# Query projections over 64 rows in two array halves, and the first expert's second-layer loads, dummy operands and output products moved round the routing

## The chip, the cores and the metric

The kernel runs on one core of one Trainium2 chip. The metric is device time in microseconds (us) of one execution, where lower is better. Times below come from the runs of the kernel before and from one execution of it that the hardware profiler recorded.

## What is computed

Three blocks follow each other over T = 2304 tokens (4 sequences of 576) and 512 channels (8 heads of 64).

```python
def phi(x):                                   # q, k: [4, 8, 576, 64], w_phi: [64, 128]
    proj = np.einsum('bhsd,df->bhsf', x, w_phi)
    proj = proj - np.max(np.abs(proj), axis=-1, keepdims=True)
    return np.concatenate([np.exp(proj), np.exp(-proj)], axis=-1)
q_p, k_p = (phi(q), phi(k))
kv = np.einsum('bhsf,bhsd->bhfd', k_p, v);  z = np.sum(k_p, axis=2)
x = (q_p @ kv) / (q_p @ z + 1e-6)             # linear attention, then [4, 576, 512]
gate = sigmoid(causal_conv5(x, conv_w))
y = (gate * (x @ w_val)) @ w_out              # gated block
e[s] = argmax(y @ w_gate) where sigmoid(y @ w_local) < 0.5 or s == 0, else e[s-1]
out[s] = softmax(y @ w_gate)[e] * (relu(y @ w1[e]) @ w2[e])   # 8 experts, 512 -> 1024 -> 512
```

## The kernel before, in words

Tokens are worked on in 18 tiles of 128. The kernel has five stretches.

**Keys.** For each tile and each half of the heads (`hh`), `proj` (L115) multiplies the raw k by the feature map `wraw`, which holds `w_phi` twice on its diagonal, so that one product of 128 rows (two heads' channels) by 256 columns serves two heads. VectorE takes the largest magnitude (L132, tile `m`) and subtracts it (L134, tile `pp`), ScalarE makes both exponentials, and `kv` (L159) sums keys times values in 64-column products.

**Queries and the gated block.** For q, `split` (L105) first makes a rounded high part of a raw tile on ScalarE (`qkh`) and the rest of it on GpSimd (`qkl`); both are of the type fp32r, which TensorE streams faster than fp32. `proj` then issues three products of 128 rows by 256 columns for each pair of heads: `qkh` by `wb_hi`, `qkh` by `wb_lo`, `qkl` by `wb_hi`, so 6 for each half of a tile and 12 for a tile. The result `pj` of a half fills one bank of PSUM; the pool `ps_p` has two. `tq` transposes (L186, tile `tp`), `nm` (L198, tile `num`) multiplies by the sums of the keys in 64-column products (16 in the program for each half; an fp32 product shows as two records in the trace), `tx` (L225) transposes back, and `conv`, `val` (L400, tile `vps`) and `ymm` (L535, tile `yps`) are the gated block. The program's order on each engine is set by a scheduler that places instructions when the ones they need are ready.

**Routing.** Products of `ymm` that are left over are called one at a time by `yfill(n)` between the short dependent steps that choose experts and build the index tables (L680 to L757). `yfill(999)` puts all that remain ahead of the last of these, `tab`. `pin` keeps those instructions in the program's order.

**Handover.** After `tab`, 30 dummy products (`idle`, L762; operands `ones` and `ohl`, a one-hot table of the routing) keep TensorE busy while the tables are finished. Tiles of the routing and of the gated block then give up their memory to the experts' weights, so that a tile of the experts waits for the last reader of what lay there.

**Experts.** Units of 256 or 384 gathered tokens. `gather` (L815) fetches rows by index on GpSimd's queue; `rows` transposes them (L827, `xp`) and splits them into `xh` and `xl`; `unit` does the first layer (L857, `hp`; `hh` and `hlo` leave it) and the second (L871, `op`). Weights come as 8 pieces of 512 KB for each expert (4 of `w1`, 4 of `w2`; L801, tile `wraw`, 3 buffers, on SP's queue); each piece is split by ScalarE (`w1h`, `w2h`) and VectorE (`w1l`, `w2l`). Before the first unit all 8 pieces of its expert are asked for and split in a row; those of expert i+1 are split at eight points inside unit i (`between`).

Of the kernel before, what the change touches and what calls it, by code (L numbers as in the profile page):

```python
# [8 lines left out]
F32 = mybir.dt.float32  # L9
F32R = mybir.dt.float32r  # L10
# [21 lines left out]
WARM = 30  # L32
# [5 lines left out]
def body(ctx, tc, qT, kT, v1, wbd, w_val, conv_w, w_out, w_gl, w1, w2, out):  # L38
# [42 lines left out]
    wb_hi = ap.tile([128, 256], F32R, name="wb_hi")  # L81
    wb_lo = ap.tile([128, 256], F32R, name="wb_lo")

    raw_t, hl_t, v_t = {}, {}, {}
# [20 lines left out]
    def split(nm, t):  # L105

        if t >= NT or (nm, t) in hl_t or nm == "k":
            return
        hi = ap.tile([128, 4, 128], F32R, tag="qkh", name="qkh", bufs=2)
        lo = ap.tile([128, 4, 128], F32R, tag="qkl", name="qkl", bufs=2)  # L110
        hi_of(A, hi, raw_t[nm, t])
        lo_of(G, lo, raw_t[nm, t], hi)
        hl_t[nm, t] = (hi, lo)

    def proj(nm, t, hh):  # L115
        raw = raw_t[nm, t]
        if nm == "k" and hh == 1:
            pj = ps_b.tile([128, 4, 128], F32, tag="b", name="pj")
        else:
            pj = ps_p.tile([128, 4, 128], F32, tag="pj", name="pj")  # L120
        for cc in range(2):
            c = 2 * hh + cc
            o = pj[:, 2 * cc:2 * cc + 2, :].rearrange("p h f -> p (h f)")
            prods = ((raw, wraw),)
            if (nm, t) in hl_t:
                hi, lo = hl_t[nm, t]
                prods = ((hi, wb_hi), (hi, wb_lo), (lo, wb_hi))
            for i, (st, mv) in enumerate(prods):
                PE.matmul(o, lhsT=st[:, c, :], rhs=mv, start=(cc == 0 and i == 0),  # L129
                          stop=(cc == 1 and i == len(prods) - 1), skip_group_check=True)  # L130
        m = ap.tile([128, 4], F32, tag="m", name="m", bufs=3)
        V.tensor_reduce(m, pj, axis=AX.X, op=ALU.max, apply_absolute_value=True)  # L132
        pp = ap.tile([128, 4, 128], F32, tag="pp", name="pp", bufs=3)
        V.tensor_tensor(pp, pj, m.unsqueeze(2).to_broadcast([128, 4, 128]), ALU.subtract)  # L134
        return pp
# [469 lines left out]
    def run(nbg, rate):  # L605
        n = len(items)
        txq = []
        for i in range(-LF, n + 3):
# [5 lines left out]
            if 0 <= i + LF < n:  # L614
                kind, t, hh = items[i + LF]
                if hh == 0:
                    loads_to(ahead[i] + 3)
                    for z in order[:ahead[i] + 2]:
                        split(*z)
                if kind == "k":  # L620
                    pk(t, hh)
                else:
                    pq(t, hh)
# [19 lines left out]
    hi_of(V, wb_hi, wraw)  # L643
    lo_of(V, wb_lo, wraw, wb_hi)
# [34 lines left out]
    yfill(18)  # L679
# [81 lines left out]
    for _ in range(WARM):  # L761
        pin(PE.matmul(idle, lhsT=rc["ones"], rhs=ohl[:, 0:4, :].rearrange("p t c -> p (t c)"), start=True, stop=True))  # L762
# [48 lines left out]
    def gather(gcols):  # L811
        xs = []
        for gc in gcols:
            xg = fx.tile([128, YW], F32, tag="xg", name="xg", bufs=XG)
            G.indirect_dma_start(out=xg, out_offset=None, in_=y_d, in_offset=bass.IndirectOffsetOnAxis(ap=gc, axis=0))  # L815
            xs.append(xg)
        return xs
# [79 lines left out]
    with tc.issue_after(W["tap"].ins), tc.issue_after(W["tanh"].ins):  # L897
        for p in pieces:
            p()()
    xs = gather(cols(gidx, units[0][0], units[0][1]))  # L900
    cur_x = rows(xs, unit_probs(0))
    xs = {1: gather(cols(gidx, units[1][0], units[1][1]))}
    for i, (c0, n, e) in enumerate(units):
# [3 lines left out]
        if not last:  # L907
            nxt["w"], pieces = unit_weights(i + 1)
            started = [p() for p in pieces[:3]]
            todo = pieces[3:]  # L910

        def between():
            if not last and started:
# [59 lines left out]
```

## Time and profile before

| | us |
|---|---|
| median of 3 runs | 597.88 (596.02 to 600.78) |
| the profiled execution | 596.02 |
| its span, first to last instruction | 594.2 |
| TensorE busy in the span | 569.9 |

The profiled execution is the fastest of the three runs, 1.86 us below their median, and 1.8 us of it lie outside the span. All times of rows count from the span's start. TensorE is PE in rows, its weight loads PEld, VectorE DVE, ScalarE ACT, GpSimd POOL. A matmul's record holds its latency, so records that follow each other overlap: what one costs is the distance from its start to the next one's.

### The profile page before, as it was taken

What the parts mean: (1) busy time and instruction counts of PE and PEld (TensorE: products, weight loads), DVE (VectorE), ACT (ScalarE), POOL (GpSimd) and SP (SyncE); (2) the same over time, 40 slices, a digit from 0 to 9 for tenths busy, and PEclk for the clock granted to TensorE, in tenths of its full rate; (3) what the DMA queues carried; (4) which work ended last, traced back from release to release, by engine and by line L of the source; (5) the groups of instructions that cost most, each with busy time, mean ns of one, the idle gap of its engine ahead of it and who ended that gap; (6) DMA issues with size and microseconds to landing.
All of it is one profiled execution on the core that took longest, in us unless ns stands there. A gap on an engine that the chain in (4) does not pass through costs nothing. (4 is left out here: it accounts for less than half of the span.)

```text
span 594.2 us, 13524 instructions
## 1 busy us (share of the span) xinstructions
PE 569.9 (96%) x5477; PEld 495.5 (83%) x5478; DVE 365.2 (61%) x726; ACT 313.1 (53%) x573; POOL 238.0 (40%) x258
## 2 busy tenths in 40 slices
PE   7999999999999999999997999999999999999993
PEld 6777788898889889888784988889889899898982
DVE  5888689478687876569613766555666656452110
ACT  3767566466665575565323656445655646541210
POOL 2453055388778885583124022322340322311001
PEclk9999999899999999999998899999999999999997
DMA  8934431111101000221524887758668649620000
GB/s 281 311 99 122 130 107 49 32 33 38 36 4 35 3 38 21 72 77 48 198 90 132 302 268 217 239 190 269 210 211 272 202 138 291 203 95 36 17 19 36
DMA packets 46017, 76.82 MB, mean 129 GB/s; under 512 B 3839, under 2 KB 22399, under 8 KB 45952
## 3 DMA queue, kind: packets, MB, share of 16 engines
q1 hardware_dynamic: 39840, 60.55, 32.8%
q0 software_dynamic: 3520, 10.58, 4.7%
q10 hardware_dynamic: 2592, 4.79, 2.1%
q8 instruction: 45, 0.74, 0.5%
q14 instruction: 20, 0.16, 0.1%
HBM read 66.39 MB, written 10.56 MB: 130 GB/s over the span
## 5 line engine op out<-in xcount | busy, mean ns | idle before, releaser
L857 PE MATMUL hp<-xh,w1h 128*128 128x256 f32 (+1 forms) x320 | 94.6, 296 | 1.4 <-DVE hlo L860 0.8
L857 PE MATMUL hp<-xh,w1l 128*128 128x256 f32 (+1 forms) x320 | 93.8, 293 | 0.0
L857 PE MATMUL hp<-xl,w1h 128*128 128x256 f32 (+1 forms) x320 | 93.3, 294 | 0.0
L815 POOL DMA_INDIRECT xg<-y_d,gidx x22 | 36.7, 1669 | 98.5 <-DVE p L838 83.4
L877 POOL DMA_INDIRECT out<-osb,sidx x22 | 28.0, 1271 | 115.1 <-ACT osb L876 69.0
L871 PE MATMUL op<-w2h,hh 128*128 128x512 f32 x176 | 69.5, 400 | 1.0 <-ACT hh L859 0.9
L52 DVE TENSOR_TENSOR w2l<-wraw,w2h 128x1024 fp32r<-128x1024 f32 x40 | 48.8, 1223 | 34.5 <-ACT w2h L49 34.3
L860 DVE SCALAR_TENSOR_TENSOR hlo<-hp,hh 128x256 fp32r<-128x256 f32 (+1 forms) x80 | 34.2, 446 | 55.4 <-ACT hh L859 55.4
L871 PE MATMUL op<-w2l,hh 128*128 128x512 f32 x176 | 68.2, 393 | 0.0
L871 PE MATMUL op<-w2h,hlo 128*128 128x512 f32 x176 | 67.0, 394 | 0.0
L857 PEld LDWEIGHTS hp<-xh,w1h 128*128 128x128 f32 x320 | 61.2, 191 | 3.9 <-DVE hlo L860 1.2
L52 DVE TENSOR_TENSOR w1l<-wraw,w1h 128x1024 fp32r<-128x1024 f32 x40 | 48.7, 1251 | 24.1 <-ACT w1h L49 24.1
L857 PEld LDWEIGHTS hp<-xh,w1l 128*128 128x128 f32 x320 | 61.1, 191 | 1.4
L857 PEld LDWEIGHTS hp<-xl,w1h 128*128 128x128 f32 x320 | 60.7, 191 | 0.0
L132 DVE TENSOR_REDUCE m<-pj 128x4 f32<-128x512 f32 x72 | 49.3, 686 | 18.4 <-PE pj L129 17.5
L266 DVE SCALAR_TENSOR_TENSOR acc<-xT,tfs,acc 128x256 f32<-128x256 f32 (+1 forms) x112 | 53.8, 485 | 10.8 <-ACT acc L264 9.7
L859 ACT ACTIVATE hh<-hp 128x256 fp32r<-128x256 f32 (+1 forms) x80 | 31.4, 403 | 53.8 <-PE hp L857 53.6
L49 ACT CAST w2h<-wraw 128x1024 fp32r<-128x1024 f32 x40 | 41.8, 1050 | 31.7 <-DMA wraw<-w 22.3
L49 ACT CAST w1h<-wraw 128x1024 fp32r<-128x1024 f32 x40 | 40.3, 1049 | 24.6 <-DMA wraw<-w 24.5
L159 PEld LDWEIGHTS kv<-v,ex 128*64 128x64 f32 (+1 forms) x1280 | 40.7, 137 | 14.7 <-issue 6.8
L134 DVE TENSOR_TENSOR pp<-pj,m 128x512 f32<-128x512 f32 x72 | 49.4, 686 | 4.4 <-PE tp L186 1.8
L159 PE MATMUL kv<-v,ex 128*64 128x65 f32 (+1 forms) x1280 | 46.1, 224 | 3.0 <-DVE kvsb L171 1.4
(194 smaller groups left out, 1332.5 us busy)
## 6 DMA issues: line engine op xcount, KB each, us to landing
wraw<-w SPq DMA_DIRECT2D x80, 512.0 KB, 4.5
v<-v SPq DMA_DIRECT2D x18, 260.0 KB, 3.2
y_d<-ysb ACTq DMA_DIRECT2D x18, 260.0 KB, 2.1
raw<-qT SPq DMA_DIRECT2D x18, 256.0 KB, 2.9
raw<-kT SPq DMA_DIRECT2D x17, 256.0 KB, 4.2
wr<-w_val SPq DMA_DIRECT2D x4, 512.0 KB, 5.9
wr<-w_out SPq DMA_DIRECT2D x4, 512.0 KB, 6.9
xg<-y_d,gidx POOLq DMA_INDIRECT x22, 5.4
```

What stands on the lines that cost most here:

```text
L49: (A.copy if eng is A else eng.tensor_copy)(hi, src)
L52: eng.tensor_tensor(lo, src, hi.bitcast(F32), ALU.subtract)
L132: V.tensor_reduce(m, pj, axis=AX.X, op=ALU.max, apply_absolute_value=True)
L134: V.tensor_tensor(pp, pj, m.unsqueeze(2).to_broadcast([128, 4, 128]), ALU.subtract)
L159: PE.matmul(kv_ps[b][blk // 7][mh * 64:mh * 64 + 64, (blk % 7) * VW:(blk % 7 + 1) * VW], lhsT=kp_t[t, hh][off:off + n, sg, h, mh * 64:mh * ...
L266: W["tap"] = V.scalar_tensor_tensor(acc[c], xs, cw[:, kk, c:c + 1], acc[c], ALU.mult, ALU.add)
L815: G.indirect_dma_start(out=xg, out_offset=None, in_=y_d, in_offset=bass.IndirectOffsetOnAxis(ap=gc, axis=0))
L857: PE.matmul(hp[:, 0:n], lhsT=wt[:, k, f * 128:(f + 1) * 128], rhs=xt[:, k, 0:n], start=(i == 0), stop=(i == 11))
L859: A.activation(hh[:, f, 0:n], hp[:, 0:n], AF.Relu)
L860: low = V.scalar_tensor_tensor(hlo[:, f, 0:n], hp[:, 0:n], 0.0, hh[:, f, 0:n].bitcast(F32), ALU.max, ALU.subtract)
L871: PE.matmul(op, lhsT=ht[:, f, sl], rhs=wt[:, f, :], start=(i == 0), stop=(i == 23))
L877: G.indirect_dma_start(out=out, out_offset=bass.IndirectOffsetOnAxis(ap=scols[j], axis=0), in_=osb, in_offset=None, bounds_check=T - 1, oo ...
```

## The change

Four things change.

1. The query projection uses raw fp32 operands and no split. The host orders the heads so that a block of 128 channels holds head c in rows 0 to 63 and head c+4 in rows 64 to 127. At the first half of a tile, 8 products of 64 rows by 128 columns are written, alternating between the upper and the lower half of the rows (`z`), into both banks of `ps_p`. The 18 ScalarE casts `qkh`, the 18 GpSimd subtractions `qkl` and the two splits of `wraw` go.
2. `yfill(18)` becomes `yfill(24)` ahead of the first routing transpose.
3. The 30 dummy products of 512 columns become 60 of 256 columns, with the identity matrix as both operands.
4. The first expert's `w2` pieces are asked for behind the first gather and split inside the first unit; the next expert's pieces start two `between` points later.

```diff
-    def split(nm, t):
-        if t >= NT or (nm, t) in hl_t or nm == "k":
-            return
-        hi = ap.tile([128, 4, 128], F32R, tag="qkh", name="qkh", bufs=2)
-        lo = ap.tile([128, 4, 128], F32R, tag="qkl", name="qkl", bufs=2)
-        hi_of(A, hi, raw_t[nm, t])
-        lo_of(G, lo, raw_t[nm, t], hi)
-        hl_t[nm, t] = (hi, lo)
+    def products(nm, t, hh):
+        raw = raw_t[nm, t]
+        if nm == "k":
...
+        elif hh == 0:
+            for z in range(2):
+                pj_t[z] = ps_p.tile([128, 4, 128], F32, tag="pj", name="pj")
+            for c in range(4):
+                for z in range(2):
+                    rows = slice(z * 64, z * 64 + 64)
+                    PE.matmul(pj_t[z][:, c, :], lhsT=raw[rows, c, :], rhs=wraw[rows, z * DF:z * DF + DF],
+                              start=(c == 0), stop=(c == 3), skip_group_check=True)
     def proj(nm, t, hh):
...
-            if (nm, t) in hl_t:
-                hi, lo = hl_t[nm, t]
-                prods = ((hi, wb_hi), (hi, wb_lo), (lo, wb_hi))
...
+        products(nm, t, hh)
+        pj = pj_t.pop(hh)
...
-    yfill(18)
+    yfill(24)
...
-        pin(PE.matmul(idle, lhsT=rc["ones"], rhs=ohl[:, 0:4, :].rearrange("p t c -> p (t c)"), start=True, stop=True))
+        pin(PE.matmul(idle[:, 0:256], lhsT=ident.bitcast(BF16)[:, 0:128], rhs=ident.bitcast(BF16), start=True, stop=True))
...
-        for p in pieces:
+        for p in pieces[:4]:
             p()()
     xs = gather(cols(gidx, units[0][0], units[0][1]))
+
+    with tc.issue_after(W["gather"].ins):
+        late = [p() for p in pieces[4:7]]
+    late_todo = pieces[7:]
...
-            started = [p() for p in pieces[:3]]
-            todo = pieces[3:]
+            started = [p() for p in pieces[:0 if i == 0 else 3]]
+            todo = pieces[len(started):]
 
         def between():
-            if not last and started:
+            if late:
+                for _ in range(2):
+                    late.pop(0)()
+                    if late_todo:
+                        late.append(late_todo.pop(0)())
+                if not late:
+                    started.extend(todo.pop(0)() for _ in range(3))
+            elif not last and started:
```

On TensorE, early in the query stretch, a half of a tile had six products of the same shape before (the number in a name tells tiles of one name apart):

```order
L198 MATMUL num_1478<-kvsb_526,ex_1434 64x65 x16
L129 MATMUL pj_1599<-wb_hi_94,qkh_1414 128x256
L129 MATMUL pj_1599<-wb_lo_95,qkh_1414 128x256
L129 MATMUL pj_1599<-wb_hi_94,qkl_1415 128x256
L129 MATMUL pj_1599<-wb_hi_94,qkh_1414 128x256
L129 MATMUL pj_1599<-wb_lo_95,qkh_1414 128x256
L129 MATMUL pj_1599<-wb_hi_94,qkl_1415 128x256
L186 MATMUL tp_1546<-ident_61,pp_1427 128x128 x4
```

At the same place of the changed kernel, the two results of one tile (`pj_1507` from the upper rows of `raw_1270`, `pj_1508` from the lower) stand apart, four products of one half in a row:

```order
L120 MATMUL pj_1507<-wraw_93,raw_1270 128x128 x4
L193 MATMUL num_1454<-kvsb_522,ex_1417 64x65 x16
L120 MATMUL pj_1508<-wraw_93,raw_1270 128x128 x4
L181 MATMUL tp_1521<-ident_61,pp_1410 128x128 x4
L120 MATMUL pj_1610<-wraw_93,raw_1337 128x128 x4
L193 MATMUL num_1529<-kvsb_522,ex_1450 64x65 x15
```

The source alternates the halves; the scheduler has put the four products of the one half ahead of the four of the other.

On TensorE, late in the query stretch, among products of `ymm` and `val`, before:

```order
L535 MATMUL yps_3662<-wout_h_238,gl_2224 128x512
L129 MATMUL pj_3679<-wb_hi_94,qkh_3435 128x256
L129 MATMUL pj_3679<-wb_lo_95,qkh_3435 128x256
L129 MATMUL pj_3679<-wb_hi_94,qkl_3436 128x256
L129 MATMUL pj_3679<-wb_hi_94,qkh_3435 128x256
L129 MATMUL pj_3679<-wb_lo_95,qkh_3435 128x256
L129 MATMUL pj_3679<-wb_hi_94,qkl_3436 128x256
L400 MATMUL vps_3729<-xh_3111,wval_h_236 128x256
```

and in the changed kernel:

```order
L530 MATMUL yps_3124<-wout_h_234,gl_1882 128x512
L120 MATMUL pj_3143<-wraw_93,raw_2682 128x128
L120 MATMUL pj_3144<-wraw_93,raw_2682 128x128
L120 MATMUL pj_3143<-wraw_93,raw_2682 128x128
L120 MATMUL pj_3144<-wraw_93,raw_2682 128x128
L120 MATMUL pj_3143<-wraw_93,raw_2682 128x128
L120 MATMUL pj_3144<-wraw_93,raw_2682 128x128
L120 MATMUL pj_3143<-wraw_93,raw_2682 128x128
L120 MATMUL pj_3144<-wraw_93,raw_2682 128x128
L220 MATMUL xp_3165<-ident_61,x_2942 128x128 x2
```

Here the two halves of one tile alternate, as written. Over the whole program 5 of the 18 query tiles alternate throughout, one does in its last four products, and 12 stand four and four.

On ScalarE, at the handover, before (what an instruction waits for stands behind it):

```order
L49 CAST w2h<-wraw 128x1024 [waits DVE_49,PE_49]
L49 CAST w2h<-wraw 128x1024 x2
L49 CAST xh<-xp 128x4x128 [waits PE_49] x2
L49 CAST w2h<-wraw 128x1024 [waits DMAHW3_49]
L49 CAST w1h<-wraw 128x1024 [waits DMAHW4_49]
```

and in the changed kernel:

```order
L49 CAST w2h<-wraw 128x1024 [waits DVE_49]
L49 CAST w2h<-wraw 128x1024 x2
L49 CAST w2h<-wraw 128x1024 [waits DMAHW3_49]
L49 CAST xh<-xp 128x4x128 [waits PE_49] x2
L49 CAST w1h<-wraw 128x1024 [waits DMAHW4_49]
```

The casts no longer wait for TensorE, and all four of the first expert's second layer stand ahead of the first rows' `xh`. On SP's queue the order of the loads is the same as before.

## Rows read from the trace of the kernel before

**Rows 1.** The page: span, and each engine's busy time

```profile
span 594.2 us, 13524 instructions
PE 569.9 (96%) x5477; PEld 495.5 (83%) x5478; DVE 365.2 (61%) x726; ACT 313.1 (53%) x573; POOL 238.0 (40%) x258
```

**Rows 2.** Busy time in a stretch: length, PE, PEld, DVE, ACT, POOL, clock, DMA

```profile
121.00:240.00 119.00, 118.29 (x1485) 104.73 (x1485) 92.36 (x232) 72.97 (x161) 95.49 (x112) 1.00 0.09 26
```

**Rows 3.** The query projection's line, stretch 121 to 240: whom it waited for

```profile
L129 PE MATMUL pj<-wb_hi,qkh x48: 276/281/393, 121.9 to 237.5; 128*128 128x256 f32 x48
...
  DVE pp L134: 2.0, 5
```

**Rows 4.** The split of q: groups by line, busy us, mean ns, idle before

```profile
L49 ACT CAST qkh<-raw 128x512 fp32r<-128x512 f32 x18 | 11.3, 630 | 3.0 <-POOL tmw L323 1.2 <-PE pj L129 1.0 <-issue 0.4
L52 POOL TENSOR_TENSOR qkl<-raw,qkh 128x512 fp32r<-128x512 f32 x18 | 24.0, 1332 | 4.9 <-ACT qkh L49 4.9
```

**Rows 5.** TensorE in order of time at 189 us: start, length, instruction

```profile
188.15 0.60 PE L225 MATMUL xp<-ident,x 128*128 128x128 f32 x4
...
189.46 0.28 PE L129 MATMUL pj<-wb_lo,qkh 128*128 128x256 f32 x1
...
190.64 0.28 PE L129 MATMUL pj<-wb_hi,qkl 128*128 128x256 f32 x1
```

**Rows 6.** TensorE in order of time at 181 us

```profile
181.30 0.28 PE L400 MATMUL vps<-xl,wval_h 128*128 128x256 f32 x1
181.51 1.15 PE L198 MATMUL num<-kvsb,ex 128*64 128x65 f32 x32
182.60 0.65 PE L186 MATMUL tp<-ident,pp 128*128 128x128 f32 x4
```

**Rows 7.** Groups by line and form: the keys' products over 64 rows

```profile
L159 PE MATMUL kv<-v,ex 64*64 64x65 f32 x256 | 9.0, 220 | 1.4 <-DVE kvsb L171 0.8 <-ACT kvsb L171 0.6
```

**Rows 8.** The handover, all engines in order of time

```profile
314.04 0.20 DVE L764 TENSOR_SCALAR tk<-tab 128x40 f32<-128x40 f32 x1 [14.52 <-PE tab L757]
...
314.81 0.20 DVE L768 TENSOR_TENSOR sidx<-tk,tk 128x40 int32<-128x40 f32 x1
318.31 1.20 POOL L815 DMA_INDIRECT xg<-y_d,gidx  x1 [10.23 <-DMA y_d<-ysb]
320.51 2.94 ACT L49 CAST w2h<-wraw 128x1024 fp32r<-128x1024 f32 x3 [6.54 <-PE idle L762]
320.76 0.94 POOL L815 DMA_INDIRECT xg<-y_d,gidx  x1 [1.24 <-PE idle L762]
321.65 3.50 DVE L52 TENSOR_TENSOR w2l<-wraw,w2h 128x1024 fp32r<-128x1024 f32 x3 [6.63 <-ACT w2h L49]
321.97 0.66 PE L827 MATMUL xp<-ident,xg 128*128 128x128 f32 x4 [1.50 <-DMA xg<-y_d,gidx]
...
322.90 2.61 SPq L801 DMA_DIRECT2D wraw<-w  x3
...
324.10 1.12 PE L827 MATMUL xp<-ident,xg 128*128 128x128 f32 x4 [1.47 <-DMA xg<-y_d,gidx]
...
325.89 0.58 PE L857 MATMUL hp<-xh,w1h 128*128 128x256 f32 x1 [0.68 <-ACT xh L49]
```

**Rows 9.** Weight loads and gathers, us from issue to landing: loads' median, gathers' min, median, max

```profile
wraw<-w SPq DMA_DIRECT2D x80, 512.0 KB, 4.5
...
DMA to landing us min/median/max: 3.3/5.4/8.5
```

**Rows 10.** Busy time by stretch, where TensorE's clock was halved

```profile
108.80:112.21 3.41, 3.41 (x26) 3.26 (x26) 1.46 (x4) 0.98 (x3) 0.00 (x0) 0.50 0.19 53
...
323.84:330.66 6.82, 5.89 (x26) 5.36 (x27) 4.87 (x6) 3.27 (x6) 3.85 (x3) 0.50 0.96 342
```

**Rows 11.** TensorE's two later waits in the first two units

```profile
366.57 0.39 PE L857 MATMUL hp<-xh,w1h 128*128 128x256 f32 x1 [0.77 <-DVE hlo L860]
...
381.44 0.50 PE L871 MATMUL op<-w2h,hh 128*128 128x512 f32 x1 [0.93 <-ACT hh L859]
```

More of the change, by code (lines that the diff above doesn't have):

```diff
@@ L31 @@
 YLAG = 4
-WARM = 30
+WARM = 60
 XG = 6
@@ L80, in body @@
     wraw = ap.tile([128, 256], F32, name="wraw")
-    wb_hi = ap.tile([128, 256], F32R, name="wb_hi")
-    wb_lo = ap.tile([128, 256], F32R, name="wb_lo")
-    raw_t, hl_t, v_t = {}, {}, {}
+    raw_t, v_t = {}, {}
     def load(nm, t):
@@ L103, in load_v @@
         SP.dma_start(v_t[t], v1[t * 128:(t + 1) * 128, :])
-    def split(nm, t):
-        if t >= NT or (nm, t) in hl_t or nm == "k":
-            return
-        hi = ap.tile([128, 4, 128], F32R, tag="qkh", name="qkh", bufs=2)
-        lo = ap.tile([128, 4, 128], F32R, tag="qkl", name="qkl", bufs=2)
-        hi_of(A, hi, raw_t[nm, t])
-        lo_of(G, lo, raw_t[nm, t], hi)
-        hl_t[nm, t] = (hi, lo)
-    def proj(nm, t, hh):
[L116 to L124, printed above, removed]
-            if (nm, t) in hl_t:
-                hi, lo = hl_t[nm, t]
-                prods = ((hi, wb_hi), (hi, wb_lo), (lo, wb_hi))
-            for i, (st, mv) in enumerate(prods):
-                PE.matmul(o, lhsT=st[:, c, :], rhs=mv, start=(cc == 0 and i == 0),
-                          stop=(cc == 1 and i == len(prods) - 1), skip_group_check=True)
+    pj_t = {}
+    def products(nm, t, hh):
+        raw = raw_t[nm, t]
+        if nm == "k":
+            pool, tag = ((ps_p, "pj"), (ps_b, "b"))[hh]
+            pj = pj_t[hh] = pool.tile([128, 4, 128], F32, tag=tag, name="pj")
+            for cc in range(2):
+                o = pj[:, 2 * cc:2 * cc + 2, :].rearrange("p h f -> p (h f)")
+                PE.matmul(o, lhsT=raw[:, 2 * hh + cc, :], rhs=wraw, start=(cc == 0), stop=(cc == 1), skip_group_check=True)
+        elif hh == 0:
[6 more added lines that the diff above has]
+                              start=(c == 0), stop=(c == 3), skip_group_check=True)
+    def proj(nm, t, hh):
+        products(nm, t, hh)
+        pj = pj_t.pop(hh)
         m = ap.tile([128, 4], F32, tag="m", name="m", bufs=3)
@@ L617, in run @@
                     loads_to(ahead[i] + 3)
-                    for z in order[:ahead[i] + 2]:
-                        split(*z)
                 if kind == "k":
@@ L642, in body @@
     loads_to(1)
-    hi_of(V, wb_hi, wraw)
-    lo_of(V, wb_lo, wraw, wb_hi)
     route_consts()
@@ L814, in gather @@
             xg = fx.tile([128, YW], F32, tag="xg", name="xg", bufs=XG)
-            G.indirect_dma_start(out=xg, out_offset=None, in_=y_d, in_offset=bass.IndirectOffsetOnAxis(ap=gc, axis=0))
+            W["gather"] = G.indirect_dma_start(out=xg, out_offset=None, in_=y_d,
+                                               in_offset=bass.IndirectOffsetOnAxis(ap=gc, axis=0))
             xs.append(xg)
@@ L947, with chan @@
     from concourse.bass_utils import run_bass_kernel_spmd
-    def chan(a):
+    def chan(a, paired=False):
+        if paired:
+            a = a[:, [h // 2 + h % 2 * (H // 2) for h in range(H)]]
         return np.ascontiguousarray(a.transpose(1, 3, 0, 2).reshape(H * DH, T))
```

2 lines of the change are left out of this document (1 added, 1 removed).

## The prediction

> **What bounds the kernel now.** I read the page first: TensorE is busy 569.9 of 594.2 us, and no other engine passes 61% [rows 1]. The table by stretch then shows where that share is a real bound. In the query stretch, from 121 to 240 us, TensorE is busy 118.29 of 119.00 us at full clock, while VectorE, ScalarE and GpSimd stand at 78, 61 and 80% [rows 2]. The projection's own line waits 2.0 us there, five times, always for VectorE's `pp`, never for the splits on ScalarE or GpSimd [rows 3]. So the query stretch costs what TensorE's instructions cost, and the 11.3 us of `qkh` and 24.0 us of `qkl` [rows 4] lie beside it. The timeline of the handover is the one place where TensorE stands still: the dummies end at 320.5, the first rows arrive at 321.97 and 324.10, and the first expert product starts at 325.89 [rows 8]. The clock is halved there from 323.84 to 330.66, and once earlier from 108.80 to 112.21 [rows 10].
>
> **The query projection, product by product.** Before: ten spacings from 189.46 to 190.64 us, so 0.118 us for a product of 128 rows by 256 columns [rows 5]. A tile has 12, all tiles 216: 25.5 us.
>
> After: products of 64 rows by 128 columns in fp32. An fp32 product is two records (the program's `num` x16 is x32 in the trace). For a record of 128 fp32 columns I use the transposes: four in 0.60 us, the last 0.28 long, so (0.60 - 0.28)/3 = 0.107 us each [rows 5]. That a contraction over 64 rows is no quicker, and no slower for its weight loads, is seen in the keys' 64-row products: 9.0 us for 256 records, 0.035 each [rows 7], beside 0.030 for the 128-row `num` (1.15 us for 32, the last 0.225 long: 0.925/31) [rows 6]. So a product alone costs 0.214 us.
>
> What two array halves give at once no row shows for rows. For columns `num` shows it: 65 fp32 columns alone would take 65/128 of 0.107, 0.054 us, and two records of opposite column halves take 0.060 together. By that a pair of products over opposite row halves costs 2 x 0.107 x 1.1 = 0.235 us instead of 0.428. Bounds: 0.214 (fully at once) to 0.428 (not at once); I take 0.235, nearest to `num`.
>
> But a pair must stand side by side, and TensorE takes its instructions in order. In the changed order 5 tiles alternate, one does for its last four products, and 12 have four products of one half and then, apart, four of the other. A serial tile costs 8 x 0.214 = 1.71 us, more than the 12 x 0.118 = 1.42 of before; an alternating one 4 x 0.235 = 0.94; the mixed one 0.86 + 0.47 = 1.33. Sum: 12 x 1.71 + 5 x 0.94 + 1.33 = 26.6 us against 25.5: **+1.1 us**.
>
> **Changes of the array's shape.** Going from full-array products into 64-column ones costs 0.21 instead of 0.12 from 181.30 to 181.51, so 0.09 us; coming out, the last `num` starts at 181.51 + 0.925 = 182.435 and the transpose at 182.60, 0.165 instead of 0.030, so 0.135 us [rows 6]. That is 0.11 us for one change. Before, `pj` was full-array; now it is a shape of its own, between neighbours that mostly are not. Counted from the first query projection to `tab`, the order has 122 changes before and 142 after: 20 x 0.11 = **+2.2 us**. Bounds: zero, if a shape of 64 rows costs nothing to enter or leave, to 4.5, if each change costs both prices.
>
> Together +3.3 us on an engine that is busy throughout. Part of it fills waits for `pp` [rows 3]; I take 0.7 of those 2.0 us: **+2.6 us** for the stretch. Taking 35.3 us of casts from ScalarE and GpSimd [rows 4] I cost at nothing, since TensorE waits for neither; bounds 0 to -2.0, all waits of [rows 3]. Its cover is gone only where GpSimd or ScalarE would be the last to deliver, which makes the change no dearer. The dropped splits of `wraw` at the start lie on VectorE, ahead of keys that TensorE multiplies raw: nothing.
>
> **yfill(24) and the dummies.** Six products of `ymm` go ahead of the first routing transpose. They are the same work earlier, and VectorE waited 14.52 us for `tab` at the end of the routing [rows 8], so a later start by six products is covered; zero. Sixty dummies of 256 columns stream as many columns as 30 of 512 and end where they did; if they take up to 1.5 us more, the wait for the first rows (320.5 to 321.97) covers it; zero.
>
> **The handover.** Before, `w2h` and the second gather wait for the last dummy, to 320.51 and 320.76 [rows 8]. Now the casts wait only for VectorE, whose table is done at 315.0 (314.81 + 0.20), so `w2h` runs from about 315 to 318 (2.94 us for three) and the fourth piece is asked for after the first `w2l`, about 317.4 instead of 322.90; two pieces of the next expert follow at 318.6 and 319.8. The second gather can be issued at 318.31 + 1.20 + 0.30 = 319.8. But the loads, now 5 us earlier, fall on both gathers. The first gather took 3.66 us on a quiet queue (318.31 to 321.97), the second 3.34; the median of all 22, mostly amid weight loads, is 5.4 and the largest 8.5 [rows 9]. With 5.4 the second lands at 325.2 instead of 324.10. The way from there to the first expert product is 1.79 us [rows 8], 1.35 without the slow clock. Bounds: 319.8 + 3.34 + 1.35 = 324.5 (-1.4 us) to 319.8 + 8.5 + 1.79 = 330.1 (+4.2). I take 319.8 + 5.4 + 1.4 = 326.6, **+0.7 us**. Queued behind `xh` on ScalarE is all of the unit, and ahead of it now stands the fourth `w2h`, which waits for its load: 317.4 + 4.5 (the loads' median) [rows 9] + 1 us of cast is 322.9, ahead of the second rows, so it costs nothing unless that load takes over 6 us.
>
> The slow clock: from 325.89 to 330.66 expert products ran at half speed, 2.4 us lost. TensorE is idle as long as before, so I keep it: 0, bounds -2.4 (no drop) to +1.7 (3.41 us more at half clock, as [rows 10] shows once). The waits at 365 and 380 us, 0.77 and 0.93 us [rows 11], come from ScalarE standing at a cast whose load is late; loads that start 5 us earlier may spare half: **-0.8 us**, bounds -1.7 to +1.7.
>
> **Sum.** +2.6 + 0.7 - 0.8 = +2.5 us on the profiled execution's 596.02: 598.5 us. That execution was 1.86 us below the median of the runs, so the time that I expect of a median is 600.4 us, 0.4% above 597.88.
>
> **The rivals.**
> *The halves do not run at once* (slower). Place: the 5 alternating tiles and the half of a sixth. Price: 5 x (1.71 - 0.94) + 0.39 = 4.2 us, time 604.6. It decides from a pair above 0.40 us. For it: no row shows opposite row halves; against: columns do it [rows 6].
> *Weight loads take turns with products of the same rows* (slower). Then each record of a serial tile costs twice 0.107: 12 x 16 x 0.107 = 20.5 us, time 621. [...] Against it: transposes that all use the same 128 rows stand 0.107 apart [rows 5], and the 64-row records 0.035 [rows 7].
> *The handover opens and the query stretch sheds its waits* (faster). Gathers on a quiet queue (-1.4), no slow clock (-2.4), both later waits gone (-1.7) and the waits for `pp` gone (-2.0), with shape changes at half price (-1.1): 597.88 + 3.3 - 8.6 = 592.6, and 591 if the clock's drop at 108.80 goes too (-1.7). For it: the casts no longer wait for the dummies; against: the loads they release.
> *The pairing works everywhere although the order is serial*: 18 x 0.94 = 16.9 us, 9.7 less, time 590.7. Against it: four products of the same rows cannot overlap each other, and `pj` of the other half stands behind 16 `num`.
>
> **How the numbers follow.** Three runs of one kernel lie within 0.8%, so about 1% is what a measurement can tell from no change: 591.9 to 603.9. My forecast has a chance of 0.58, and nearly all of its spread stays within 1%. Slower: halves not at once 0.15, turns 0.03, more slow clock or a dear gather 0.04, together 0.22. Faster: the open handover with a lighter stretch 0.16, the pairing 0.04, together 0.20. The range takes in the first slower rival and most of the faster one: 591.5 to 606.5; the forecast's own is 596 to 604.
>
> **What would show it.** Right: `pj` records of serial tiles 0.107 apart and of alternating ones in pairs a few ns apart, about 27 us in all; the first `w2h` near 315 on the old count, gathers of over 4.5 us at the handover, and `hp` no sooner after VectorE's first step on `tab` than the 11.85 us of before. Wrong: a query stretch shorter than before by more than 2 us, a handover without a halved clock, or `pj` records 0.2 apart.

## The result, and the profile after

The changed kernel takes 606.88 us in the median of 14 executions (600.42 to 616.55), beside 597.89 us (594.70 to 600.78) for the kernel before, 1.5% more. The ratios in this document leave out executions over 1.5% above the fastest of their kernel: here six of the 14, the profiled one of 614.08 us among them, below e7's profiled one, e1's longest and a few far off (637 and 791 us in e3, 797 and 3090 us in the kernel before). By that ratio the change costs 1.2% (1.0124, 95% interval 1.0091 to 1.0157). Because the executions lie so far apart, a second profile of the same program stands beside the first below (e11, 603.82 us), and wherever a sum is made, it is made with that one. Predicted were 600.4 us, 0.4% more, with 596 to 604 as the forecast's own range and 591.5 to 606.5 as the whole one: the median lies above both, 0.4 us above the second.

The page of the changed kernel, against [rows 1]:

```profile
span 612.4 us, 13678 instructions
PE 583.7 (95%) x5580; PEld 508.6 (83%) x5580; DVE 360.8 (59%) x724; ACT 303.4 (50%) x555; POOL 211.7 (35%) x240
```

ScalarE and GpSimd lost their casts (10 and 26 us less), VectorE 4 us. TensorE is busy for 14 us more, although no work of that size was added. The table by stretch says why (columns as in [rows 2]; the clock is the third from the right):

```profile
88.00:94.76 6.76, 5.45 (x121) 4.91 (x119) 5.67 (x10) 3.51 (x7) 2.48 (x2) 1.00 0.27 79
94.76:111.83 17.07, 17.07 (x117) 14.82 (x117) 7.57 (x15) 4.36 (x9) 3.80 (x3) 0.50 0.11 32
111.83:115.24 3.41, 3.41 (x30) 3.12 (x30) 1.40 (x4) 1.82 (x5) 0.00 (x0) 1.00 0.03 7
115.24:128.90 13.66, 13.66 (x105) 12.39 (x105) 4.29 (x10) 3.37 (x9) 1.26 (x1) 0.50 0.07 19
128.90:255.30 126.40, 124.97 (x1651) 109.86 (x1651) 95.59 (x243) 72.48 (x163) 85.61 (x103) 1.00 0.10 29
328.87:343.87 15.00, 9.15 (x88) 7.56 (x87) 6.30 (x11) 5.81 (x8) 7.20 (x6) 0.89 0.70 246
```

For 17.07 and again 13.66 us TensorE ran at half clock (granted clock 0.50; the records of a serial tile stand 0.213 to 0.215 us apart there and 0.112 where the granted clock is 1.00), against one stretch of 3.41 us before [rows 10]. In those stretches it is busy all the time, VectorE for 7.57 and 4.29 us of them, so TensorE is the bound there. The first product of `vps` comes at 135.74 instead of 121.01 us; from there to `tab` only 1 us more is lost.

What TensorE did before the clock fell, in order of time:

```profile
87.77 1.16 PE L120 MATMUL pj<-wraw,raw 64*128 64x128 f32 x16
88.86 3.01 PE L154 MATMUL kv<-v,ex 128*64 128x65 f32 x94
93.19 1.13 PE L120 MATMUL pj<-wraw,raw 64*128 64x128 f32 x8 [1.31 <-issue]
94.25 0.33 PE L154 MATMUL kv<-v,ex 128*64 128x65 f32 x2
94.50 0.33 PE L181 MATMUL tp<-ident,pp 128*128 128x128 f32 x1
94.76 2.07 PE L120 MATMUL pj<-wraw,raw 64*128 64x128 f32 x8
```

The first query tile takes both banks of `ps_p` at once. The second tile has to wait until VectorE is done with the first of them; TensorE runs ahead with the keys' products that are left (`kv` x94), has nothing to do for 1.31 us, and then gets products of one half of the rows. The idle time says "issue", but the first weight load after the gap starts at 93.16 us, ahead of its product at 93.19, and the queue for weight loads holds one wait of 2.09 us among this line's rows (minimum, median and maximum in ns):

```profile
L120 PE MATMUL pj<-wraw,raw x288: 271/272/580, 87.8 to 252.9; 64*128 64x128 f32 x144
L120 PEldq EVENT_SEMAPHORE  x13: 51/51/2093, 87.1 to 190.8; - x13
...
  issue: 5.3, 11
  DVE pp L129: 1.7, 3
```

That wait ends at 93.13 us, behind VectorE's first `pp` of the first tile. On VectorE, between `m` and `pp`, stands a step of 1.1 us that has nothing to do with the projection (`tbw`, which prepares weights of the gated block):

```profile
90.19 1.28 DVE L127 TENSOR_REDUCE m<-pj 128x4 f32<-128x512 f32 x2
91.38 1.10 DVE L313 SCALAR_TENSOR_TENSOR tbw<-wr,tfw 128x512 int32<-128x512 int32 x1
92.41 1.27 DVE L129 TENSOR_TENSOR pp<-pj,m 128x512 f32<-128x512 f32 x2
```

It is nearly as long as TensorE's idle time; no run moved it.

The handover, against [rows 8]:

```profile
329.73 0.20 DVE L755 TENSOR_SCALAR tk<-tab 128x40 f32<-128x40 f32 x1 [13.14 <-PE tab L748]
...
330.73 2.94 ACT L49 CAST w2h<-wraw 128x1024 fp32r<-128x1024 f32 x3 [1.07 <-DVE sidx L759]
...
332.70 1.46 POOL L806 DMA_INDIRECT xg<-y_d,gidx  x1 [8.92 <-ACT w2h L49]
333.12 16.49 SPq L792 DMA_DIRECT2D wraw<-w  x6
334.47 1.71 POOL L806 DMA_INDIRECT xg<-y_d,gidx  x1 [0.30 <-issue]
...
339.12 0.66 PE L819 MATMUL xp<-ident,xg 128*128 128x128 f32 x4 [2.88 <-DMA xg<-y_d,gidx]
...
342.08 1.11 PE L819 MATMUL xp<-ident,xg 128*128 128x128 f32 x4 [2.30 <-DMA xg<-y_d,gidx]
...
343.87 0.58 PE L849 MATMUL hp<-xh,w1h 128*128 128x256 f32 x1 [0.67 <-ACT xh L49]
```

The casts, the first load and the second gather start earlier after `tab`, as forecast, but the two gathers take 6.4 and 7.6 us to land, where before they took 3.6 and 3.3. From `tab` to the first `hp` it is 15.00 us instead of 12.71.

### The profile page after: what moved, and what is told of

Its sections match the earlier page's. It is cut to its first block, busy times and chain, and to the rows that moved or that the text cites. A ratio compares the mean times of both kernels' runs of the same rounds, so it can differ in the third digit from the quotient of the medians.

```text
span 612.4 us, 13678 instructions
## 1 busy us (share of the span) xinstructions
PE 583.7 (95%) x5580; PEld 508.6 (83%) x5580; DVE 360.8 (59%) x724; ACT 303.4 (50%) x555; POOL 211.7 (35%) x240
## 5 line engine op out<-in xcount | busy, mean ns | idle before, releaser
L806 POOL DMA_INDIRECT xg<-y_d,gidx x22 | 34.2, 1554 | 101.4 <-DVE p L830 88.5
```

The lines of the kernel that those rows point to most:

```text
L806: W["gather"] = G.indirect_dma_start(out=xg, out_offset=None, in_=y_d, in_offset=bass.IndirectOffsetOnAxis(ap=gc, axis=0))
```

## The experiments

All stand in one table. The third column is the way from the last keys' product to `tab`, the fourth the time at half clock in it, the fifth the third less half of the fourth (an estimate of the way at full clock). Times in us; profiled execution and way come from the same execution; the ratio (with its 95% interval) is against the kernel before on the same chip.

| kernel | median, ratio | profiled, last `kv` to `tab` | at half clock | at full clock | `tab` to `hp` | `hp` to end |
|---|---|---|---|---|---|---|
| before | 597.9 | 596.02, 218.4 | 3.4 | 216.7 | 12.7 | 268.3 |
| changed | 606.9, 1.0124 (1.0091 to 1.0157) | 614.08, 234.5 | 30.7 | 219.2 | 15.0 | 268.5 |
| e11 changed, again | 603.6, 1.0099 (1.0062 to 1.0137) | 603.82, 225.3 | 10.2 | 220.2 | 15.1 | 267.7 |
| e1 projection alone | 610.4, 1.0175 (1.0112 to 1.0239) | 610.08, 234.4 | 30.7 | 219.1 | 12.3 | 268.0 |
| e2 the rest alone | 596.7, 1.0005 (0.9973 to 1.0036) | 594.17, 216.8 | 0 | 216.8 | 14.1 | 267.3 |
| e5 one bank at a time | 607.6, 1.0182 (1.0124 to 1.0240) | 605.82, 228.7 | 6.8 | 225.3 | 15.0 | 265.9 |
| e6 dummies in the gap | 601.0, 1.0082 (1.0048 to 1.0115) | 599.88, 220.9 | 6.8 | 217.5 | 14.4 | 267.2 |
| e7 old dummies | 610.3, 1.0165 (1.0103 to 1.0226) | 612.65, 234.6 | 30.7 | 219.2 | 12.4 | 269.9 |
| e4 128 rows, fp32 | 602.8, 1.0093 (1.0058 to 1.0128) | 600.92, 221.5 | 0 | 221.5 | 13.8 | 269.3 |
| e3 chained pairs | 596.3, 0.9974 (0.9944 to 1.0003) | 596.27, 217.7 | 0 | 217.7 | 14.9 | 268.8 |
| e8 chained pairs, rest as before | 595.4, 0.9968 (0.9938 to 0.9997) | 593.84, 219.2 | 3.4 | 217.5 | 12.5 | 267.3 |
| e9 as e8, three banks | 597.4, 0.9993 (0.9953 to 1.0032) | 597.39, 219.8 | 10.2 | 214.6 | 12.7 | 268.8 |
| e10 as e8, dummies in the gap | 599.5, 1.0033 (0.9990 to 1.0077) | 598.92, 220.6 | 10.2 | 215.5 | 12.9 | 268.0 |
| e12 as e9, dummies at `wps` | 595.0, 0.9953 (0.9925 to 0.9981) | 595.08, 216.7 | 0 | 216.7 | 12.9 | 267.7 |

The theory (A): the new projection leaves TensorE short of work after the keys, and the halved clock that follows is the loss. The rivals: the later parts cause it (B), fp32 without a split does (C), products over 64 rows do whatever their order (D).

Each kernel was profiled once, the changed one twice. But the span and the mean granted clock of every execution are on record, and from them the time at half clock in a whole execution, handover and end included, can be estimated: twice the missing share of the clock times the span (43 us for the first profile, where its stretches add up to 45). It is 18 to 50 us for the changed kernel's 14 executions, and 11 to 28 for those of the kernel before that the experiments' ratios count. This estimate is used below where one profile says too little.

**e1 and e2, the parts apart.** e1 is the kernel before with only the projection of the change; e2 is the changed kernel with the split projection of before.

```diff
-            prods = ((raw, wraw),)
-            if (nm, t) in hl_t:
-                hi, lo = hl_t[nm, t]
-                prods = ((hi, wb_hi), (hi, wb_lo), (lo, wb_hi))
...
+                    PE.matmul(pj_t[z][:, c, :], lhsT=raw[rows, c, :], rhs=wraw[rows, z * DF:z * DF + DF],
+                              start=(c == 0), stop=(c == 3), skip_group_check=True)
```

(e1 makes this edit in the kernel before, e2 takes it back in the changed one.)

> Part 1 alone: the kernel before with the new query projection; yfill, dummies and weight loads as before. Theory A (the new projection is what leaves TensorE short of work after the keys, 90 to 94 us, while VectorE empties both banks of a tile, and the halved clock follows from that): the profile shows the granted clock halved for more than 7 us between 90 and 130 us, the first value product (vps) later than the 121.0 us of before, the way from tab to the first hp within 0.5 us of the 12.7 of before, and a median of 600 to 606 us that differs from execution to execution by several us. Rival B (the later parts cause the loss): the first vps within 1.5 us of 121.0, the time within 2 us of before.

> Parts 2 to 4 alone: the changed kernel with the old split projection. Theory A: the stretch up to 130 us is that of before (first vps near 121.0, one drop of the clock of 3.4 us), the handover from tab to the first hp takes about 15.0 us instead of 12.7, because the weight loads released early share the DMA engines with the two gathers; time +1.5 to +2.5 us, 599.5 to 600.5 of a median of 598. Rival B: 603 to 607, with the drop of the clock in the query stretch as in the changed kernel.

e1, by stretch:

```profile
88.00:93.70 5.70, 4.39 (x108) 4.03 (x104) 5.11 (x9) 2.89 (x6) 1.71 (x2) 1.00 0.22 60
93.70:127.83 34.13, 34.13 (x248) 30.04 (x247) 13.30 (x28) 9.23 (x21) 5.06 (x4) 0.55 0.08 24
```

The projection alone brings the slow stretch (clock 0.55 over 34 us, 1.31 us idle ahead of it) and the whole loss and more (610.4 us, where 600 to 606 were expected), with the handover as before (12.3). e2 keeps full clock through the query stretch and pays 1.4 us at the handover, yet its time is that of before: the expected +1.5 to 2.5 us did not show in the total. B falls.

**e11, the changed kernel again.**

> The changed kernel as it is, for an execution of its own beside the candidates. Theory A: the execution's time follows the length of the halved clock between 88 and 130 us at half a microsecond for a microsecond: with 30.7 us as in its first profile about 612 to 614, with 6.8 us about 601 to 602; the way from tab to the first hp is 14 to 15 us in either case.

```profile
88.00:95.43 7.43, 6.12 (x125) 5.53 (x121) 6.31 (x10) 3.59 (x7) 2.13 (x2) 1.00 0.22 63
95.43:98.84 3.41, 3.41 (x17) 3.01 (x15) 1.87 (x4) 2.15 (x5) 0.05 (x1) 0.50 0.28 82
98.84:109.08 10.24, 10.24 (x128) 8.98 (x127) 6.26 (x14) 4.03 (x10) 3.74 (x3) 1.00 0.10 28
109.08:115.91 6.83, 6.83 (x52) 6.64 (x50) 1.64 (x5) 0.75 (x3) 0.00 (x0) 0.50 0.13 38
```

The same instructions in the same order, the same idle 1.3 us, and the clock falls at the same place, but comes back after 3.41 us instead of 17.07. Between the two executions the way to `tab` differs by 9.2 us and the half-clock time in it by 20.5; half of that is 10.2. The 14 executions of the first result say the same: the longer the estimated time at half clock, the longer the execution, by 0.42 us for each microsecond (correlation 0.92). So the changed kernel's time follows its half clock. Three of the 14 have hardly more of it than the profile of the kernel before (18 to 20 us, there 18); they take 600.4 to 602.8 us.

**e5 and e6, what lets the clock fall.** e5 gives each half of a tile its own turn (one bank, all products of one half of the rows, nothing side by side), so that keys and projections alternate as before. e6 leaves the change as it is and writes 14 dummy products ahead of the second query tile.

```diff
+            z = hh
+            pj_t[z] = ps_p.tile([128, 4, 128], F32, tag="pj", name="pj")
+            rows = slice(z * 64, z * 64 + 64)
+            for c in range(4):
+                PE.matmul(pj_t[z][:, c, :], lhsT=raw[rows, c, :], rhs=wraw[rows, z * DF:z * DF + DF],
+                          start=(c == 0), stop=(c == 3), skip_group_check=True)
```

```diff
+        if nm == "q" and hh == 0 and t in (1,):
+            idle = ps_b.tile([128, 512], F32, tag="b", name="hold")
+            for _ in range(14):
+                PE.matmul(idle[:, 0:256], lhsT=ident.bitcast(BF16)[:, 0:128], rhs=ident.bitcast(BF16), start=True, stop=True)
```

> The changed kernel with one bank at a time: four products of the upper 64 rows at the first half of a tile, four of the lower at the second, none side by side. The order of TensorE's work after the keys is then that of before, with keys' products between the projections. Theory A (TensorE has nothing to do from 91.9 to 93.2 us because one tile holds both banks, and that lets the clock fall): no halved clock beyond 3.4 us between 88 and 130 us; every half of a tile costs 1.085 us, 39 us in all instead of the 31.6 of before, so 7.5 us more plus 1.4 to 2.3 at the handover: 604 to 608, with executions close together. Theory D (products over 64 rows that don't run in pairs are too little work for the clock, whatever the order): halved for more than 7 us between 88 and 130 us, and over 609.

> The changed kernel with 14 dummy products of 256 columns (0.112 us each, 1.6 us in all) written ahead of the second query tile, where TensorE stood idle for 1.3 us. Theory A: no halved clock beyond 3.4 us between 88 and 130 us, first vps at 119 to 123 us instead of 135.7, executions close together, time 598 to 602. Theory D: the clock falls all the same, some us later, first vps after 128, time 604 to 610.

e5 by stretch, then e6 in order of time:

```profile
88.00:107.24 19.24, 19.24 (x262) 16.78 (x262) 14.73 (x26) 9.58 (x20) 5.75 (x5) 1.00 0.19 52
107.24:114.07 6.83, 6.83 (x54) 6.56 (x55) 1.46 (x4) 0.43 (x3) 0.00 (x0) 0.50 0.13 38
```

```profile
88.33 2.09 PE L158 MATMUL kv<-v,ex 128*64 128x65 f32 x64
90.34 1.70 PE L110 MATMUL hold<-ident 128*128 128x256 bf16 x14
91.98 0.56 PE L158 MATMUL kv<-v,ex 128*64 128x65 f32 x10
92.64 1.77 PE L124 MATMUL pj<-wraw,raw 64*128 64x128 f32 x16
```

In e5 TensorE is busy 19.24 of 19.24 us, and the clock holds until 107 us although no two projection products of 64 rows run side by side: in this profile D falls for the drop at 94 us. The time of the profiled execution is what the products cost: 225.3 us at full clock, 8.6 more than before where 7.5 were expected. But its executions do not lie close together, as A expected (605.0 to 613.4 us, three of six above the 609 of D), and the two longest are at half clock for 6 to 10 us more than the profiled one; where, no profile shows. In e6 the gap is gone and the drop near 94 us with it. With 1.6 us of useless products it takes 1.0082 times the time before, beside 1.0124 and, on the same chip, 1.0099 for the changed kernel; the intervals overlap, so the gain is not clear of the noise. The dummies also shifted the order (the second tile now runs in pairs), so e6 by itself does not tell the two apart. In both the clock falls near 107 us, for 6.83 us where A expected no more than 3.4; that place is taken up with e12.

**e7, the dummies.** The changed kernel with the 30 dummies of before.

```diff
-        pin(PE.matmul(idle[:, 0:256], lhsT=ident.bitcast(BF16)[:, 0:128], rhs=ident.bitcast(BF16), start=True, stop=True))
+        pin(PE.matmul(idle, lhsT=rc["ones"], rhs=ohl[:, 0:4, :].rearrange("p t c -> p (t c)"), start=True, stop=True))
```

> The changed kernel with the 30 dummy products of before (operands ones and the one-hot table), so that the casts of w2 wait for their end as before. If the loads released early are what slows the gathers, the way from tab to the first hp is 12.3 to 13.0 us instead of 15.0; the query stretch is as in the changed kernel, halved clock included in some executions; time 2 us below the changed kernel's, about 604 to 605 in the median. If the moved w2 loads cost by themselves, the way stays above 14 us and the time at 606 to 607.

```profile
332.50 1.20 POOL L806 DMA_INDIRECT xg<-y_d,gidx  x1 [8.92 <-DMA y_d<-ysb]
335.99 2.94 ACT L49 CAST w2h<-wraw 128x1024 fp32r<-128x1024 f32 x3 [6.54 <-PE idle L753]
336.13 0.66 PE L819 MATMUL xp<-ident,xg 128*128 128x128 f32 x4 [0.17 <-DMA xg<-y_d,gidx]
336.24 0.94 POOL L806 DMA_INDIRECT xg<-y_d,gidx  x1 [2.53 <-DMA xg<-y_d,gidx]
...
338.38 6.86 SPq L792 DMA_DIRECT2D wraw<-w  x4
...
339.72 0.66 PE L819 MATMUL xp<-ident,xg 128*128 128x128 f32 x4 [2.93 <-DMA xg<-y_d,gidx]
```

With the casts behind the dummies again, the first load is asked for at 338.38, after the first gather has landed; both gathers take 3.6 and 3.4 us, and the way is 12.4 us. So the dearer gathers of the changed kernel come from the loads beside them. The other profiles agree: where the first load is asked for within half a microsecond of the first gather (e2 to e6, e11), the first two gathers take 4.8 to 7.7 us as far as their landing is recorded; where it comes after both (e1, e8, e9, e10, e12), 3.2 to 3.7. The time did not fall by 2 us, though: this kernel keeps the early half clock (30.7 us in its profile), and `hp` to the end is 1.4 us longer. What the handover is worth in the total is therefore not shown; e2 says not much.

**e3, e8 and e4, other forms of the projection.** e3 chains the 8 products of a tile (each may only be placed behind the one before) and begins with the lower half, so that the halves of the rows should stand in pairs in all tiles (106 of 144 possible pairs of records start within 0.02 us of each other, 56 in the changed kernel); e8 is the same projection with the rest as before. e4 uses raw fp32 in the keys' form, 128 rows, one bank at a time.

```diff
-            for c in range(4):
-                for z in range(2):
+            mm = None
+            for c in range(4):
+                for z in (1, 0):
                     rows = slice(z * 64, z * 64 + 64)
-                    PE.matmul(pj_t[z][:, c, :], lhsT=raw[rows, c, :], rhs=wraw[rows, z * DF:z * DF + DF],
-                              start=(c == 0), stop=(c == 3), skip_group_check=True)
+                    with ExitStack() as es:
+                        if mm is not None:
+                            es.enter_context(tc.issue_after(mm.ins))
+                        mm = PE.matmul(pj_t[z][:, c, :], lhsT=raw[rows, c, :], rhs=wraw[rows, z * DF:z * DF + DF],
+                                       start=(c == 0), stop=(c == 3), skip_group_check=True)
```

```diff
+        pool, tag = ((ps_p, "pj"), (ps_b, "b"))[hh if nm == "k" else 0]
+        pj = pj_t[hh] = pool.tile([128, 4, 128], F32, tag=tag, name="pj")
+        for cc in range(2):
+            o = pj[:, 2 * cc:2 * cc + 2, :].rearrange("p h f -> p (h f)")
+            PE.matmul(o, lhsT=raw[:, 2 * hh + cc, :], rhs=wraw, start=(cc == 0), stop=(cc == 1), skip_group_check=True)
```

> The changed kernel with the 8 products of a query tile chained, so that a product of the lower and one of the upper half of the rows stand side by side in all 18 tiles. A tile then costs 1.09 us (measured on the alternating tiles) instead of 2.17, so TensorE's projection falls from 31 to about 20 us at full clock. If TensorE's length of work sets the query stretch, the time is 8 to 11 us below the changed kernel, 592 to 598. Theory A' (VectorE holds both banks, TensorE waits, the clock falls): waits for VectorE's pp grow from 1.7 to over 5 us, the clock still falls between 90 and 130 us, and the time is 600 to 606.

> The kernel before with the new projection alone and its products chained in pairs: a candidate to beat both. The query stretch of the chained kernel ended 2.2 us earlier than that of before (tab at 310.9), and the handover of before costs 12.3 to 12.7 us instead of 14.9: time 592 to 595, 3 to 5 us below before. Rival: the 2 us at the handover come back as waits in the first two units, and the time is 596 as with the chained products in the changed kernel.

> The changed kernel with the query projection in the form of the keys: raw fp32, 128 rows by 256 columns, two products for a half of a tile, and one bank of PSUM at a time, no split. By the keys' rows a half costs 0.96 to 1.06 us instead of the 0.88 (31.6 us over 36) of the split, +3 to +6 us on TensorE, plus the handover's 2.3. Theory A (two banks at once and 64 rows starve TensorE, not fp32 itself): no drop of the clock beyond the 3.4 us of before between 90 and 130 us, first vps 121 to 124, time 600 to 605 with little spread. Rival C (raw fp32 without the split is enough to lower the clock): clock halved for over 7 us between 90 and 130 us, vps after 128, time over 605.

e3, the stretch and the projection's waits:

```profile
88.00:130.00 42.00, 38.70 (x599) 34.42 (x595) 30.44 (x68) 22.34 (x48) 18.55 (x20) 1.00 0.15 44
```

```profile
L124 PEldq EVENT_SEMAPHORE  x18: 51/51/2081, 86.6 to 219.3; - x18
...
  DVE pp L133: 6.0, 8
```

The pairs save 4.9 us of `pj` (26.5 us in e3 and e8, 31.4 before, summed over the starts of its records up to what follows), but TensorE now idles for 5.6 us up to `tab` instead of 2.3 (2.3 us of it for `pp` and 1.3 in the gap behind the keys; the 6.0 of the line count its weight loads' waits too), and `tp`, `xp` and `vps` cost 3.5 us more between them: at full clock the way is 0.8 to 1.0 us longer than before and 1.5 to 2.7 shorter than the changed kernel's. The wait of 2.08 us of the changed kernel is still there, yet the clock holds beyond it, in e3 to the handover and in e8 to 105 us. So in these profiles neither the gap alone (e3, e8) nor the separate halves alone (e5) let the clock fall at 94 us; the four profiles that have both (changed, e11, e1, e7) show the fall, between 93.7 and 95.4 us. The executions of e3 and e8 bear this out: by the estimate those in the ratios have 13 to 21 and 11 to 24 us at half clock, no more than those of the kernel before. Why it takes both, no run shows; the chain also changes what follows the gap, and even with both, three of the changed kernel's 14 executions have hardly more half clock than the kernel before. e4 holds full clock from 88 us to the handover too and costs what its products cost (4.8 us more at full clock, 3 to 6 expected): C falls. e8, which was to beat the kernel before by 3 to 5 us, is 0.3% faster (0.03 to 0.62%), about 2 us.

**e9, e10 and e12, a version that beats both.** e9 gives the projection a third bank, taken from the pool of `xp`, `vps` and `yps`; e10 writes 12 dummies into the gap of e8, as e6 did; e12 is e9 with four dummies ahead of each of the four groups of 9-column products (`wps`).

```diff
-    ps_p = psx.enter_context(tc.tile_pool(name="ps_p", bufs=2, space=PSUM))
+    ps_p = psx.enter_context(tc.tile_pool(name="ps_p", bufs=3, space=PSUM))
...
-    ps_b = psx.enter_context(tc.tile_pool(name="ps_b", bufs=3, space=PSUM))
+    ps_b = psx.enter_context(tc.tile_pool(name="ps_b", bufs=2, space=PSUM))
```

```diff
-                        wps = ps_b.tile([128, E + 1], F32, tag="b", name="wps")
+                        full = ps_b.tile([128, 512], F32, tag="b", name="wps")
+                        wps = full[:, 0:E + 1]
+                        for j in range(4):
+                            for _ in range(1):
+                                PE.matmul(full[:, 256:512], lhsT=ident.bitcast(BF16)[:, 0:128], rhs=ident.bitcast(BF16), start=True, stop=True, skip_group_check=True)
```

> The chained pairs alone (rest as before), with three banks for the projection's pool and two instead of three for the pool of xp, vps and yps. If the 5.9 us that the projection waits for VectorE's pp come from a tile needing both banks of two, a third bank halves them and tab comes 2 to 3 us earlier than the 312.4 of the chained pairs: 592 to 594. If VectorE itself is late, or the bank that vps and yps lose costs as much, 595 to 599.

> The chained pairs alone (rest as before) with 12 dummy products (1.3 us) ahead of the second query tile. Theory A: the 1.3 us in which TensorE stood idle there are filled, no halved clock between 90 and 130 us (3.4 us in the chained pairs' profile, 1.7 us lost), first vps at 117 to 119 us, time 593 to 595. If the drop near 105 us comes from the 9-column products (wps) alone, it stays, and the time is 595 to 597.

> The chained pairs with three banks, and ahead of each of the four groups of 9-column products (wps) four dummy products of 256 columns, 16 in all, 1.8 us. In the three-bank kernel the clock fell at 108.9 us for 10.2 us, during those 9-column products; without that its way from the last keys' product to tab is 214.7 us against 216.7 of before. If that second drop comes from the little work of the 9-column products: halved for no more than 3.4 us between 90 and 130 us, tab 3 us earlier (311), time 593 to 595. If the clock falls there all the same: tab at 316, time 598 to 600.

e10, then e12:

```profile
88.00:104.69 16.69, 16.23 (x259) 13.81 (x256) 12.32 (x24) 9.54 (x20) 5.69 (x5) 1.00 0.20 57
104.69:114.93 10.24, 10.24 (x84) 9.20 (x84) 3.25 (x7) 1.96 (x6) 0.02 (x1) 0.50 0.09 26
```

```profile
88.00:130.00 42.00, 40.14 (x629) 35.47 (x625) 30.94 (x70) 21.59 (x46) 18.60 (x20) 1.00 0.18 52
...
104.00 0.60 PE L373 MATMUL wps<-ident 128*128 128x256 bf16 x4
104.43 0.96 PE L375 MATMUL wps<-wgl,woT 128*128 128x9 f32 x8
```

e9 did not shorten TensorE's waits for `pp` (4.3 us, 2.3 in e8) and missed its 592 to 594 us. Its way would be the shortest of all at full clock, 214.6, but half clock from 108.9 us takes 5.1 of it back. e10 missed: its gap is nearly filled, and still 10.2 us at half clock come near 105 us, where TensorE works on `wps`. In the kernel before, the drop of [rows 10] begins at that work too; those of e5, e6, e8, e9 and e10 and the second one of e11 begin during the two stretches of `wps` or between them. e2, e3 and e4 pass it without one in their profiles. e12 puts 1.8 us of dummies exactly there, and from the keys to the handover no half clock is left; the way comes to 216.7 us, about what e9 would take at full clock and the dummies' 1.8 on top, and `tab` at 312.7 where 311 was expected. It is 0.5% faster than the kernel before (0.19 to 0.75%); from e8 and e3 its time is not told apart. By the estimate from the granted clock its 12 executions have 12 to 21 us at half clock in all (median 14), the six of e9 20 to 24 (median 23), so the gain in the clock is not one execution's luck.

## Why the prediction came out as it did

**The products: right.** Forecast for a serial record 0.107, a pair 0.235, 26.6 us in all. Measured: serial records 0.112 apart; where the halves alternate throughout, the two records side by side start 0.006 to 0.007 apart and the next two 0.112 after them, 0.224 from one pair of products to the next (the first of a group 0.1 later). So the halves run fully at once here: two records side by side take as long as one alone. The sums were both too small, 25.5 and 26.6 us against 31.4 and 31.7 measured, since the first record of a group costs more than those behind it; in the difference that cancels. With time at half clock counted half, the starts of e11's records from 8 us ahead of the last keys' product to `tab` add up as follows:

| us | before | e11 |
|---|---|---|
| `pj` | 31.4 | 31.7 |
| `vps`, `tp`, `xp` | 79.7 | 82.3 |
| `yps`, `num`, `lpp`, `kv` | 103.0 | 102.6 |
| idle | 2.3 | 3.2 |

Here `pj` holds its own price and the change of shape at its start and end: +0.3. The +2.6 of `vps`, `tp` and `xp`, whose products are the same as before, lies at the first and last records of their groups (+3.3 there, -0.7 at those between), so it goes with the changes of shape; no run takes those apart. The +0.9 of idle time stands where the forecast had -0.7. The forecast's +1.1 and +2.2, less 0.7, made +2.6; e11 gives +3.5 on the way to `tab` at full clock and the first profile +2.4. The halves-not-at-once rival is refuted. So is the one on weight loads: records of the same rows stand 0.112 apart, not twice 0.107, although the record of a weight load is 0.188 us long in the median (the shortest 0.182).

**The clock in the query stretch: wrong, and the step that failed.** "The slow clock" was weighed at the handover alone and kept at 0, with 3.41 us more as the bound. In the query stretch the forecast took full clock from [rows 2], which begin at 121 us, and priced the first 30 us after the keys by them; [rows 10] had a drop in just that place. It also set the waits for `pp` down as slack that the longer products fill, and did not look at the place where a tile takes both banks and TensorE has to wait for them (1.3 us). Measured: 10.2 us at half clock in e11 and 30.7 in the first profile instead of 3.4, so 3.4 to 13.7 us. The branch that named "more slow clock or a dear gather" had 0.04, and no sign under "Wrong" in the prediction points at this place. That the time still lies close to the upper end of the whole range is luck: the range reached up there for halves that do not run at once, and they do.

**The handover: right in its mechanism, mis-sized.** Casts and load came at the times forecast after `tab` (the first load 4.25 us after it, 4.2 forecast), the second gather 1 us sooner. The term was +0.7, from a second gather of 5.4 us; the second gather took 7.6 and the first, which was left at its quiet time, 6.4: +2.3. The slow clock there stayed, 6.83 us as before, but with `hp` later less of it lies behind the first `hp`: 3.5 us and, in e11, 3.3 instead of 4.8, which gives back 0.7. Later waits: forecast -0.8, and they went the other way. In place of the two waits of [rows 11], 1.7 us, TensorE stands idle for 3.1 us in the first profile and 2.9 in e11, each time for ScalarE's `hh`. The way from the first `hp` to the end is still only +0.2 and -0.7 us off that of before; what makes up the rest was not traced.

**The sum for e11.** +3.5 to `tab` at full clock, +3.4 half clock, +2.4 handover, -0.65 after it, -0.75 up to the keys' end: 7.9 us, the difference of the spans (602.1 and 594.2). Without the term of the clock it is 4.5, where 2.5 were forecast: so much of the forecast holds when the clock does.

**The rivals on the faster side** were right about the price of a pair. But chained, the projection costs 5.2 us less than in the changed kernel (26.5 and 31.7) and not 9.7, since the first products of a chain often stand alone ahead of other work. Of that gain 1.5 to 2.7 us are left on the way to `tab`, as TensorE stands idle for longer.

## What to carry to other kernels

In these runs two halves of the array paid only where the instructions stood in pairs (0.112 us for two records side by side, 0.112 for each one alone); order alone in the source does not hold them together (56 of 144 pairs of records here), a chain does so more often (106). When a step begins to take all buffers of its pool at once, look at the first place where the consumer is late and at what stands ahead of it there, and read the granted clock at that place, not in the stretch where the engine is fullest. A few cheap products can be worth more than they cost at the place where the clock falls: with 1.8 us of dummies at `wps`, e12's profile has no half clock on the way to `tab`, where e9's has 10.2 us; with 1.3 us of them in the earlier gap, e10's has 10.2 us all the same.

## What the runs showed of the hardware that was not expected

The same program, in the same order, kept half clock for 17.07 us after a drop in one execution and for 3.41 us in another; at half clock TensorE was busy without a gap in both (17.07 of 17.07 us, 3.41 of 3.41). Its executions spread over 16 us, and their granted clocks go with their times (correlation 0.92). Those of e4 and e12, whose profiles show full clock from 88 us to the handover, spread over less than 6 us, those of e2, whose profile shows the same, over 8. The clock also fell with no idle time ahead of it: in e5 at 107.24 us, after 19.24 us in which TensorE was busy throughout. A gather of 128 rows at the handover took 3.2 to 3.7 us with no weight load beside it and 4.8 to 7.7 with loads, over all profiles; in the changed kernel's first profile it was 6.4 and 7.6, at a DMA share of 0.70.
